# A new order for an attention and gated feed-forward kernel: how its planner prices loads and weights

## The chip, the cores and the metric

The kernel runs on one core of a Trainium2 chip. The metric is device microseconds of one execution, the median of several. Engines are named as in the profile: PE (TensorE: matrix products, with PEld for its weight loads), DVE (VectorE), ACT (ScalarE), POOL (GpSimd) and SP (SyncE, which here issues loads, DMA transposes and stores). Each engine carries out its own instructions in order, and waits on semaphores for the others.

## The reference

Causal attention with 16 extra keys and values ahead of the sequence ("beacons"), over 8 batches, 8 heads, 576 positions and 64 columns a head, and then a gated feed-forward layer (FFN) over the 4608 tokens:

```python
k_all = np.concatenate([beacon_k, k], axis=2)
v_all = np.concatenate([beacon_v, v], axis=2)
scores = scale * np.matmul(q, k_all.transpose(0, 1, 3, 2))
scores = np.where(causal, -1000000000.0, scores)
a = np.exp(scores - scores.max(-1, keepdims=True))
a /= a.sum(-1, keepdims=True) + 1e-09
attn = np.matmul(a, v_all)
x = attn.transpose(0, 2, 1, 3).reshape(B * S, H * D)
gate = np.maximum(x @ w_gate, 0.0)
out = (gate * (x @ w_val)) @ w_out
```

The weights are 512 x 1536 (gate and value) and 1536 x 512 (out). Inputs and output are float32 in HBM; products are in bf16 with float32 sums.

## The kernel before, in words

**Loads and casts.** A batch is brought in with 15 loads on SP's queue, named in strings like `ORDER0` (batch 0), `ORDER1` (batch 1) and `ORDER` (the others): `k0` to `k3` and `q0` to `q3` are K and Q of a pair of heads, `v0` to `v4` are V by 128 rows, `F` is the first rows of Q with the beacon keys, `L` the last rows of K and Q. Loads land in staging tiles `st` (seven). A cast makes bf16 of each (`h` for K and Q, line 486; `v`, lines 440 to 442), on POOL, in batch 0 on POOL or DVE (`CASTS`). PE turns K and Q by matmuls with an identity (`turned`, line 498), and ACT or DVE evict the result into `kT` and `diag`. Q lies in `diag` in blocks with zeros, so that one matmul gives both heads' scores.

**Attention.** For each pair of heads, `tile_step` computes blocks of scores on PE (lines 656 to 664; the last rows, "F", for all pairs together, line 659), their least value with the mask on DVE (L676, L679; Q carries a negative scale), exponentials with row sums on ACT (L690), the reciprocal on DVE (L704), and the normalisation on POOL (L711). The probabilities are then transposed, on PE in batch 0 (L746) and by DMA in the others (L757), and multiplied by V (L767, on half the columns of the array for each head; L796 for F). An eviction writes the result, transposed, into `xT`, the FFN's input, which stays on the chip. Batches 0 and 1 do this in three steps (AB, C, DE), batch 2 in two (AB, CDE), the others in one.

**FFN.** `hidden` makes 12 groups for each chunk of tokens: four matmuls with the gate weights, ReLU on ACT into `g` (L838), four with the value weights, and a product on DVE into `hT` (L842). `project` makes the output with 12 matmuls a tile (L854) in three parts, an eviction into `osb`, and a store. A batch's first 512 tokens go in one or two chunks (`CUTS`); the other 64 of each batch are gathered for four batches at a time.

**Weights.** The nine weights (g0, v0, g1, v1, g2, v2, o0, o1, o2, 1 MB each in HBM) are brought in, cast to bf16 on the way, by DMAs that POOL issues (L455) among its other instructions. Batch 1 and later batches may begin to load only when one weight, `GATE`, has landed; for batch 1 this is a true semaphore, on SP.

**The order.** All of this is entered as tasks with a cost, engines, dependencies, tiles that they hold and a priority. `Plan.order` takes the tasks one by one: the one that can begin first, by the planner's own model of the engines and of DMA, and at equal times by priority (`RANK`, `AHEAD`, `STEPS`, `F_RANK`, `WHOLE`, `HOLD`, `PACE`). Tasks with two engines go to the one that is free sooner. That sequence is the program: each engine's instructions stand in it as the planner took them, while the semaphores come from the true dependencies. A wrong cost therefore gives no wrong result, only another order. While PE would wait in the first microseconds, the planner puts fillers into its order (line 918): matmuls of 256 columns on constant data that nobody reads, which keep its clock up. They are part of the program and are carried out whether PE would have waited or not.

**The model of DMA before.** `wire` is when the loads' queue will be done; each load adds its move time. Weights are due `W_FROM + W_STEP * i`; while any is under way, a load is made slower by `PACKET` for each of its packets, and the weight by `W_DELAY`.

## Time and profile before

| | us |
|---|---|
| median of 3 runs (406.59 to 407.25) | 407.08 |
| the profiled execution: whole time | 407.43 |
| its span, from the first to the last instruction | 405.6 |
| PE busy, of the span | 393.0 |
| DVE busy | 314.6 |
| ACT busy | 289.8 |
| POOL busy | 232.6 |

A row of a timeline reads: start, duration, engine, line, operation, tile written <- tiles read, shape, count, and in brackets the idle time ahead of it with the engine and line that ended it. Matmuls overlap, so that the duration of one is its latency, and the distance between two starts is what it takes of PE. A row of the stretches reads: the stretch, its length, then busy time and (count) of PE, PEld, DVE, ACT and POOL, the granted share of PE's clock, the busy share of the DMA engines, and GB/s. In a row of groups, the busy time and the mean duration in ns are followed by the idle time ahead and what ended it.

### The profile page before, as it was taken

The numbers are of one execution on the slowest core, as the hardware profiler recorded it, in microseconds if no ns is written. First come the engines' busy times: TensorE is split into PE (matmuls) and PEld (weight loads), VectorE is DVE, ScalarE is ACT, GpSimd is POOL, SyncE is SP. The second block draws the span as 40 slices with busy tenths as digits, with TensorE's granted clock in tenths as the row PEclk, the third lists the DMA queues.
The fourth block names the chain that finished last, engine by engine and source line by source line (L and its number), as shares of the span: only waits on it lengthen the run. The fifth ranks groups of instructions, "written<-read, shape, count | busy, mean of one in ns | idle before, by whom it ended". The sixth has DMA issues, their size and how long they took to land.

```text
span 405.6 us, 10379 instructions
## 1 busy us (share of the span) xinstructions
PE 393.0 (97%) x3276; PEld 246.9 (61%) x3311; DVE 314.6 (78%) x1159; ACT 289.8 (71%) x959; POOL 232.6 (57%) x434
## 2 busy tenths in 40 slices
PE   7899999999999999998999999999999999999996
PEld 5567868587766877554557754554554545444484
DVE  6898999889989988898998998887988634233252
ACT  6899989789888968796888789998858433033030
POOL 5799876957786758686975965885736300000000
PEclk9999999999999999999999999999999999999999
DMA  8999999999899998999999999999296640110112
GB/s 223 170 202 224 210 216 198 195 239 204 187 182 241 199 191 222 190 225 202 236 199 210 230 203 174 256 181 222 81 163 126 146 95 0 53 52 0 53 52 54
DMA packets 172616, 68.03 MB, mean 168 GB/s; under 512 B 146832, under 2 KB 168080, under 8 KB 172560
## 3 DMA queue, kind: packets, MB, share of 16 engines
q1 hardware_dynamic: 167568, 62.38, 76.2%
q0 software_dynamic: 4752, 4.72, 7.2%
q8 instruction: 26, 0.43, 0.5%
q14 instruction: 30, 0.25, 0.2%
q10 hardware_dynamic: 240, 0.26, 0.2%
HBM read 38.27 MB, written 9.44 MB: 118 GB/s over the span
## 4 chain that ended last, share of the span: by engine, by line
PE 85%; POOL 6%; ACT 2%; DMA 2%; DVE 2%; issue 1%; SPq 0%; POOLq 0%; ACTq 0%; DVEq 0%
PE f L834 43%; PE f L854 22%; PE f L664 7%; PE f L767 5%; PE f L498 4%; POOL xT L711 2%; DMA st<-in_q_dram 2%; PE f L656 2%; POOL pb L711 1%; PE f L796 1%; POOL h L486 1%; PE f L746 1%; DVE diag L440 1%; PE f L659 1%; ACT xT L690 1%
## 5 line engine op out<-in xcount | busy, mean ns | idle before, releaser
L711 POOL TENSOR_SCALAR pb<-pb,small 128x576 bf16<-128x576 bf16 (+8 forms) x224 | 121.5, 557 | 55.4 <-DVE small L704 47.7
L690 ACT ACTIVATE pb<-f,small 128x64 bf16<-128x64 f32 (+6 forms) x256 | 131.0, 524 | 18.1 <-DVE small L679 14.3
L838 ACT ACTIVATE g<-f 128x512 f32<-128x512 f32 (+3 forms) x156 | 72.0, 470 | 66.8 <-PE f L834 65.6
L679 DVE CUSTOM_DVE_ANT_0 f<-f,mask 128x128 f32<-128x128 f32 (+7 forms) x256 | 111.8, 476 | 9.0 <-PE f L664 5.9
L834 PE MATMUL f<-xT,wv_r 128*128 128x512 bf16 (+3 forms) x616 | 111.8, 313 | 0.6
L842 DVE TENSOR_TENSOR hT<-g,f 128x512 bf16<-128x512 f32 (+3 forms) x156 | 80.1, 519 | 38.3 <-PE f L834 35.2
L834 PE MATMUL f<-xT,wg_r 128*128 128x512 bf16 (+3 forms) x619 | 109.5, 313 | 0.3
L854 PE MATMUL f<-wo_r,hT 128*128 128x512 bf16 (+1 forms) x423 | 101.9, 373 | 1.0
L834 PEld LDWEIGHTS <-wg_r 128*128 128x128 bf16 x624 | 60.0, 98 | 32.3 <-issue 0.2
L834 PEld LDWEIGHTS <-wv_r 128*128 128x128 bf16 x624 | 59.4, 98 | 32.9 <-issue 0.8
L854 PEld LDWEIGHTS <-hT 128*128 128x128 bf16 x444 | 41.6, 98 | 38.9
L690 ACT ACTIVATION_READ_ACCUMULATOR pb<-f,small 128x1 f32 x256 | 53.8, 210 | 0.0
L664 PE MATMUL f<-kT,diag 128*128 128x384 bf16 (+7 forms) x255 | 46.9, 286 | 2.2 <-DVE diag L440 1.0
L679 DVE DVE_READ_ACCUMULATOR2_ANT small<- 128x1 f32 x296 | 41.2, 139 | 0.2 <-issue 0.2
L486 POOL TENSOR_SCALAR h<-st 128x512 bf16<-128x512 f32 x62 | 37.7, 615 | 3.7 <-DMA st<-in_q_dram 1.0
L440 DVE COPY osb<-f 128x512 f32<-128x512 f32 (+1 forms) x26 | 17.6, 677 | 23.2 <-PE f L854 22.7
L711 POOL TENSOR_SCALAR xT<-xT,small 128x64 bf16<-128x64 bf16 (+4 forms) x64 | 26.9, 436 | 9.8 <-ACT xT L690 4.0
L498 PE MATMUL f<-ident,h 128*128 128x128 bf16 (+3 forms) x320 | 28.0, 218 | 2.1 <-POOL h L486 1.8
L664 PEld LDWEIGHTS <-diag 128*128 128x128 bf16 x256 | 20.4, 98 | 15.2 <-issue 1.6
L438 ACT CAST diag<-f 64x512 bf16<-64x512 f32 (+2 forms) x52 | 23.0, 443 | 9.3 <-PE f L498 4.1
L498 PEld LDWEIGHTS <-h 128*128 128x128 bf16 (+1 forms) x320 | 20.9, 99 | 13.9 <-POOL h L486 6.7
L440 DVE CAST diag<-f 64x512 bf16<-64x512 f32 (+2 forms) x44 | 26.3, 598 | 3.7 <-ACT diag L438 2.0
(67 smaller groups left out, 376.9 us busy)
## 6 DMA issues: line engine op xcount, KB each, us to landing
st<-in_q_dram SPq DMA_DIRECT2D x32, 256.0 KB, 4.4
st<-in_k_dram SPq DMA_DIRECT2D x32, 256.0 KB, 4.7
out_dram<-osb SPq DMA_DIRECT2D x32, 256.0 KB, 2.6
st<-in_v_dram SPq DMA_DIRECT2D x24, 256.0 KB, 4.8
st<-in_v_dram SPq DMA_DIRECT2D x8, 224.0 KB, 5.2
wg_r<-in_moe_w_gate_dram POOLq DMA_DIRECT2D x3, 512.0 KB, 8.7
wv_r<-in_moe_w_val_dram POOLq DMA_DIRECT2D x3, 512.0 KB, 9.9
wo_r<-in_moe_w_out_dram POOLq DMA_DIRECT2D x3, 512.0 KB, 13.3
```

The source lines that it names most:

```text
L438: nc.scalar.copy(dst, src)
L440: nc.vector.tensor_copy(dst, src)
L486: (nc.gpsimd if x.engine == "POOL" else nc.vector).tensor_scalar(to, of, by, 1.0, ALU.mult, ALU.mult)
L498: nc.tensor.matmul(to, h16.tile[:deep, a * P:(a + 1) * P], ident[:deep, :rows], start=True, stop=True)
L664: nc.tensor.matmul(view(i), t.diag.tile[:, p, j * P:j * P + P], kT[:, p, :n], start=True, stop=True)
L679: nc.vector.tensor_tensor_reduce(out=view(i), in0=view(i), in1=msk, scale=1.0, scalar=small["t"][:, 0:1] if name in "EF" else 3.0e38, op0= ...
L690: nc.scalar.activation(ph.tile.rearrange("p a n -> p (a n)")[:, a:a + n], view(i), AF.Exp, bias=small["t"][:, low:low + 1], scale=-1.0, ac ...
L711: (nc.gpsimd if x.engine == "POOL" else nc.vector).tensor_scalar(one, one, small["t"][:, 8 + i:9 + i], 1.0, ALU.mult, ALU.mult)
L834: nc.tensor.matmul(to, w_r[:, ki, nf * P:(nf + 1) * P], x, start=(ki == 0), stop=(ki == KM - 1))
L838: r = add("ACT", c_act(w), lambda _, psg=psg, g=g: nc.scalar.activation(g.tile[:, :w], psg.tile[:, :w], AF.Relu), (a,), (psg, g), -1000 + ...
L842: hid.append(add("DVE", c_dve(w), lambda _, psv=psv, g=g, nf=nf: nc.vector.tensor_mul(hT[nf].tile[:, c0:c0 + w], g.tile[:, :w], psv.tile[: ...
L854: nc.tensor.matmul(ps.tile[:, :w], hT[nf].tile[:, t0:t0 + P], wo_r[:, nf, n0:n0 + w], start=(nf == 0), stop=(nf == NF - 1))
```

## The change

What is computed does not change, nor any instruction's shape but those named here. The change replaces the planner's model of DMA, refits many of its costs, and takes new values for all priorities, so that the order of nearly all instructions is another.

- A class `Wire` models the loads' queue and the weights' queue: alone, a load takes its move time and a weight `W_MOVE`; together they take turns packet by packet (a weight has `W_PACKETS`). A weight's arrival is now taken from this, and tasks behind it become ready when it lands (`LANDING` after its last packet).
- Each weight has its own earliest time, `W_AT`, in place of `W_FROM + W_STEP * i`.
- Behind 60 us of planned time, each signal to a task takes 0.3 us more for PE and 0.15 for others (`SLACK`).
- In the model, F's value products are no longer of the kind that shares a tiling with the others, and F's scores are a kind of their own.
- Fillers multiply a tile of ones, written by DVE at the start, in place of identity and mask, which POOL writes; they may begin at 0.95 instead of 1.55, and until 8 us they fill a wait of PE wholly, later three quarters of it.
- Casts of batch 0 go to POOL alone; `GATE` is g1 instead of g0; the cut of batch 1's first chunk is at 368 tokens instead of 240; scores may hold five PSUM banks instead of four (`SC_MOST`), batch 0's turns and values six instead of four (`FIRST_MOST`).
- `SLOT_LAZY` and the second value of `begin` are gone; evictions of one tile's two halves are chained in the plan.

```diff
-W_FROM = 14.62
-W_STEP = 2.67
+W_AT = (13.08, 14.33, 19.39, 19.58, 33.69, 35.02, 39.54, 43.52, 48.0)
...
-GATE = ('g', 0)
-SC_MOST = 4
+GATE = ('g', 1)
+SC_MOST = 5
...
-ORDER0 = "q0 q1 F k0 k1 k3 v1 q3 k2 q2 v2 v3 L v0 v4"
-ORDER1 = "k0 F q0 k2 L k3 q2 v3 q3 k1 v0 v2 q1 v1 v4"
-ORDER = "q0 k1 L k0 F q3 k3 q1 v1 k2 v0 v4 v3 q2 v2"
+ORDER0 = "k3 k0 k2 v4 F q0 q3 k1 q1 L q2 v2 v1 v0 v3"
+ORDER1 = "k1 q0 F k2 q2 v4 q3 v1 v0 q1 k0 v3 v2 k3 L"
+ORDER = "k1 v1 q2 k0 k3 q0 F q1 q3 v4 k2 L v2 v3 v0"
...
-CASTS = ('POOL', 'DVE')
+CASTS = ('POOL',)
...
-CUTS = {0: (240,), 1: (240,), 2: (240,), 3: ()}
+CUTS = {0: (240,), 1: (368,), 2: (240,), 3: ()}
...
+class Wire:
...
+    def load(self, at, move, packets):
+        self.idle_to(at)
+        left = 1.0
+        beside, slower = move + packets * W_MOVE / W_PACKETS, W_MOVE + W_PACKETS * move / packets
+        while left > 1e-9:
+            w = self.weights[self.next] if self.next < len(self.weights) else None
+            if w is None or w[1] >= self.at + left * move:
+                self.at += left * move
+                left = 0.0
+            elif w[1] > self.at:
+                left -= (w[1] - self.at) / move
+                self.at = w[1]
+            elif w[2] * slower <= left * beside:
+                left -= w[2] * slower / beside
+                self.at += w[2] * slower
+                w[2], w[3] = 0.0, self.at
+                self.next += 1
+            else:
+                w[2] -= left * beside / slower
+                self.at += left * beside
+                left = 0.0
+        return self.at
...
+                              + (0.0 if end <= SLACK_FROM else SLACK[0] if "PE" in u.engines else SLACK[1]))
...
-                n = int((at - since) * FILL / 0.107) if at > WARM else int((at - since) * FILL0 / 0.2137)
+                rate = 0.2137 if since < WARM else 0.107
+                n = int((at - since) * FILL / 0.107) if at > FILL_COLD else math.ceil((at + FILL_PAD - since) / rate) if at > since else 0
...
+    def make_ones(_):
+        nc.vector.memset(ones, 1.0)
...
-        weight(kind, j, -21.0 + 0.1 * i, W_FROM + W_STEP * i)
+        weight(kind, j, -21.0 + 0.1 * i, W_AT[i])
...
-            nc.tensor.matmul(to[:, :256], ident, mask.bitcast(BF16)[:, :256], start=True, stop=True)
+            nc.tensor.matmul(to[:, :256], ones[:, :P], ones, start=True, stop=True)
```

## The prediction, as put on record before the changed kernel ran

> **What bounds the kernel now.** I read the page's busy line and slices first, then the chain of waits, then the busy time by stretch.

> ```profile
> span 405.6 us, 10379 instructions
> PE 393.0 (97%) x3276; PEld 246.9 (61%) x3311; DVE 314.6 (78%) x1159; ACT 289.8 (71%) x959; POOL 232.6 (57%) x434
> PE   7899999999999999998999999999999999999996
> PE 85%; POOL 6%; ACT 2%; DMA 2%; DVE 2%; issue 1%; SPq 0%; POOLq 0%; ACTq 0%; DVEq 0%
> ```
> ```profile
> 0.00:28.64 28.64, 24.07 (x221) 16.90 (x222) 24.07 (x119) 22.86 (x74) 21.65 (x49) 1.00 0.96 194
> 28.64:45.00 16.36, 15.79 (x221) 12.15 (x220) 14.54 (x55) 15.20 (x46) 16.18 (x27) 1.00 1.20 223
> 45.00:300.00 255.00, 251.88 (x2226) 164.16 (x2251) 228.31 (x869) 216.63 (x750) 183.04 (x339) 1.00 1.04 202
> 300.00:405.60 105.60, 101.30 (x611) 53.72 (x618) 47.64 (x118) 35.16 (x93) 11.76 (x22) 1.00 0.28 68
> L918 PE MATMUL f<-mask,ident 128*128 128x256 bf16 x90 | 15.5, 305 | 1.9 <-POOL mask L383 1.9
> ```

> TensorE (PE) is the bound, and its true work is the same in both kernels: the order of instructions holds the same 3221 matmuls beside the fillers (90 before, 105 after). So only three things can change: the time until PE has FFN matmuls to fill its waits with, the small costs between matmuls, and PE's waits. After 28.64 us PE idles 0.57 us until 45 and 3.12 us (255.00 - 251.88) until 300. The start is where time is lost: PE is called busy for 24.07 of 28.64 us, but most of that is fillers.

> ```profile
> 1.89 2.50 PE L918 MATMUL f<-mask,ident 128*128 128x256 bf16 x11 [1.89 <-POOL mask L383]
> 5.71 1.70 PE L918 MATMUL f<-mask,ident 128*128 128x256 bf16 x7
> 8.09 0.39 PE L498 MATMUL f<-ident,h 128*128 128x128 bf16 x4
> 8.31 0.49 PE L918 MATMUL f<-mask,ident 128*128 128x256 bf16 x3
> 8.64 0.39 PE L498 MATMUL f<-ident,h 128*128 128x128 bf16 x4
> 9.35 0.73 PE L664 MATMUL f<-kT,diag 128*128 128x64 bf16 x6 [0.32 <-ACT kT L438]
> 28.64 0.57 PE L834 MATMUL f<-xT,wg_r 128*128 128x240 bf16 x4
> ```

> A matmul's own duration is its latency; what it takes of PE is the distance to the next start. Three fillers of 256 columns take 0.33 us (8.31 to 8.64), so 0.107 each or 2400 columns per us; I count PE's work that way, with a pair of half-width value products as one. Before the first FFN matmul at 28.64 stand 8.19 us of true work, so 20.45 us are lost there.

> **The change part by part.** The change redraws the whole order, so I sum by stage.

> *A. Until the first FFN matmul.* The order of after puts 8.53 us of true work and 11.09 us of fillers (104) ahead of it. Its first scores need q0, now the sixth load (behind k3, k0, k2, v4 and F); before, q0 came first and their last load, k0, fourth. On PE, 43 fillers (4.59 us) and 1.39 us of turns stand ahead of these scores. The first eleven fillers above start every 0.21 us (1.89 to 4.18), double the 0.107 of 8.31, and the slow spacing still holds in the seven from 5.71. If PE is slow until 7.5 us as there, a start near 1.05 us (the fillers now wait for a memset on DVE alone) does 6.45 / 2 = 3.2 us of that work by 7.5, the other 2.75 by 10.25. So the first score comes no sooner than about 10.3, against 9.35.

> [...]

> ```profile
> 10.82 0.32 ACT L690 ACTIVATE xT<-f,small 128x64 bf16<-128x64 f32 x1
> 15.48 0.58 ACT L438 CAST diag<-f 64x512 bf16<-64x512 f32 x1 [1.46 <-DVE diag L440]
> 29.48 0.47 ACT L838 ACTIVATE g<-f 128x240 f32<-128x240 f32 x1
> L690 ACT ACTIVATE pb<-f,small 128x512 bf16<-128x512 f32 x4 | 2.9, 719 | 0.0
> L690 ACT ACTIVATE pb<-f,small 128x448 bf16<-128x448 f32 x2 | 1.3, 658 | 0.0
> L438 ACT COPY xT<-f 128x768 bf16<-128x768 bf16 x1 | 0.8, 819 | 0.0
> ```

> Then ACT sets the pace. From its first exponential (10.82) to its first ReLU (29.48) it took 18.66 us, 17.2 without the 1.46 wait for DVE. The order of after has 38 instructions there too: one exp of 512, one of 448 and one copy of 768 more (0.72 + 0.66 + 0.82), one exp of 320 less (some 0.55), and smaller evictions of K and Q (some 0.65 less): together about 1.0 more, 18.2. Its first exp I put 0.8 later, at 11.6: the scores are 0.95 later, ACT's own evictions ahead of them end nearer to them. 11.6 + 18.2 = 29.8 without a wait, 0.3 later than before, so FFN starts near 29.0. PE has then done 0.34 more true work. A = 0.3 - 0.34, taken as 0. Bounds: -0.5 (exp at 11.1) to +1.5 (a wait like the 1.46 again). What speaks for no wait: K and Q of all four pairs are now loaded and turned ahead of V, and DVE, whose eviction ACT waited for, loses four casts.

> ```profile
> L486 DVE TENSOR_SCALAR h<-st x2: 383/404/426, 3.7 to 9.0; 128x512 bf16<-128x512 f32 x2
> L486 POOL TENSOR_SCALAR h<-st x62: 607/617/620, 4.6 to 286.3; 128x512 bf16<-128x512 f32 x62
> ```

> Those casts (two of h, two of v) cost POOL 4 x 0.62 = 2.5 us. POOL was busy 21.65 of 28.64 us, so 7 us of idle time hide them; without that cover they would add up to 2.5.

> *B. Batch 1's loads behind the third weight.* Before, every load of batch 1 waited for the first weight (GATE g0), now for g1. SP is in order, so behind that wait stand all further loads, the transposes and the output stores.

> ```profile
> 16.04 0.93 POOL L455 DMA_DIRECT2D wg_r<-in_moe_w_gate_dram  x1
> 19.64 0.79 POOL L455 DMA_DIRECT2D wv_r<-in_moe_w_val_dram  x1
> 21.93 0.79 POOL L455 DMA_DIRECT2D wg_r<-in_moe_w_gate_dram  x1
> DMA to landing us min/median/max: 5.7/8.7/10.7
> DMA to landing us min/median/max: 6.0/9.9/12.4
> st<-in_k_dram SPq DMA_DIRECT2D x32, 256.0 KB, 4.7
> 37.93 0.39 PE L498 MATMUL f<-ident,h 128*128 128x128 bf16 x4
> ```

> The two landing rows (least, median, most) are the gate weights' and the value weights'. Before, g0 (issue 16.04, landed 5.7 later, 21.75) let the loads go, and PE asked for batch 1's first turn only near 37.9: some 11 us of cover. In after that turn stands 1.12 us of true work behind the first FFN matmul, near 30.2. On POOL stand ahead of g1 ten casts of Q and K and three of V (13 x 0.62 = 8.1), eight normalisations of 0.29 to 0.45 (3.0) and two issues (1.7); with the setup (until 3.6) and half of POOL's former waits I put its issue at 19.5. It lands at 25.2 (5.7) at best, at 28.2 (8.7, what the third weight took before) at worst; I take 6.0, the second weight's, as most of the wire is free by then: 25.5. A load of 4.7 and a cast of 0.62 with 0.1 of signal: 30.9 against 30.2. But a first FFN matmul that is itself a little late hides some, so B = +0.4; bounds 0 and 28.2 + 5.4 - 30.2 = +3.4 (5.4 being the same load and cast).

> *C. Changes of array tiling.* Value products run on half the columns, F's scores on a quarter. The row shapes of PE show what going in and out costs:

> ```profile
> 30.64 0.57 PE L834 MATMUL f<-xT,wg_r 128*128 128x240 bf16 x4
> 31.14 0.36 PE L767 MATMUL f<-xT,v 128*64 128x128 bf16 x6
> 36.19 0.53 PE L767 MATMUL f<-xT,v 128*64 128x128 bf16 x12
> 36.65 0.39 PE L918 MATMUL f<-mask,ident 128*128 128x256 bf16 x2
> ```

> Four of 240 columns from 30.64 end at 31.04, the next starts at 31.14: 0.10. Six pairs of 128 from 36.19 end at 36.51, the next starts at 36.65: 0.14. The order holds 60 such changes before and 67 after: C = 7 x 0.11 = +0.8 (0.7 to 1.0).

> *Batch 1's cut.* 240 + 272 columns become 368 + 144: the same columns and as many instructions. A 144-column matmul takes 0.060, and a turn of 128 with its own weights takes 0.055 (8.09 to 8.31), so weight loads hide: 0. Were they to show at 98 ns each, 96 x 0.038 = 3.6.

> *D. PE's waits behind the start.*

> ```profile
> 38.55 0.29 PE L498 MATMUL f<-ident,h 128*128 128x64 bf16 x4 [0.23 <-POOL h L486]
> 60.69 0.40 PE L498 MATMUL f<-ident,h 128*128 128x128 bf16 x4 [0.58 <-POOL h L486]
> 188.93 0.32 PE L498 MATMUL f<-ident,h 128*128 128x80 bf16 x4 [0.98 <-POOL h L486]
> DMA to landing us min/median/max: 5.4/10.6/14.8
> DMA to landing us min/median/max: 10.7/11.9/13.4
> ```

> The two last rows are loads of Q, K and V issued in 21 to 30 and in 37 to 50 us: with weights on the wire all that time they landed after 10.6 and 11.9 (medians) where 4.7 is usual, and the waits named at 38.55 and 60.69 are turns whose casts came late. After spaces its weights: 23 instructions of POOL, of 0.3 to 0.7 us each, stand between the fourth and the fifth, so for some 8 us the loads should have the wire alone and take about 4.7; the plan also allows 0.3 us more on each signal to PE behind 60 us. Of the idle 0.57 + 3.12 = 3.7 I take 2.4 as gained. Bounds: all 3.7 gained; or 1.6 lost, new waits as long as the two later ones here (0.58 + 0.98) on top of the old, since batch 2's first turn moves from 48.6 to 40.3 us of true work and so nearer to its loads.

> *End.* The last value product has 57 us of true work behind it before, 59 after, and the same last evictions and stores: 0.

> Sum: 0 + 0.4 + 0.8 - 2.4 = -1.2. The profiled execution took 407.43 us (span 405.6, 1.83 around it); the median is 407.08, 0.35 lower. 407.08 - 1.2 = 405.9; I say 405.8, as a part of B goes if A comes out late.

> **Rivals.**
> 1. *The gate decides (slower).* g1 lands near 28.2, PE stands at batch 1's first turn, which is in order ahead of all FFN work. For it: its cover of 11 us falls to none, and the third weight took 8.7. Against: batch 0's loads end sooner than batch 1's did, so less shares the wire. It decides from a landing past 27.3 (B = 2.5, so 408.0); at worst B = 3.4 and the time 408.9.
> 2. *Waits only change place.* D gains 1 instead of 2.4 and C stays: 407.08 + 0.4 + 0.8 - 1.0 = 407.3, no change. For it: PE idles only 1% already, and new orders bring new tight places.
> 3. *Vector work comes too early (slower).* Batch 7's first turn moves from 224 to 206 us of true work, so DVE (228.31 of 255 busy) must go faster on the way, and POOL takes casts. Each missed turn costs 0.6 to 1; D = +1.6 gives 409.9.
> 4. *The start gains too* (A = -0.5, B = 0, D = -3.7): 403.7.

> **How the numbers follow.** The forecast has 0.42, rival 1 0.25, rival 2 0.14, rival 3 0.12, rival 4 0.07. A measurement of this kernel can tell about 0.2%, 0.8 us, from no change. Faster: 0.42 + 0.07 = 0.49; same 0.14; slower 0.37. The forecast's own range is 404.2 to 406.2; for 8 in 10 it reaches to most of rivals 1 and 3 and to rival 4: 403.3 to 409.6.

> **What would show it.** First score (the six matmuls on kT and diag) at 10.2 to 10.8, first exp near 11.6, first FFN matmul at 28.5 to 29.5 (A). SP's wait for g1 ending at 25 to 26, and PE idle ahead of a turn between 29 and 32 of under 1 us (B); 2 us or more there is rival 1. Batch 1's K and Q loads landing in about 5 us, PE's idle time between 45 and 300 near 1.5 (D); over 3 us there is rival 2 or 3. I am wrong altogether if the first FFN matmul comes past 31, or if PE's idle time is less and the span is not.

## The result, and the profile after

| | before | after |
|---|---|---|
| median, us | 407.08 (406.59 to 407.25) | 409.15 (408.23 to 410.52, 5 runs) |
| ratio of after to before, 95% interval | | 1.0054 (1.0028 to 1.0079) |
| the profiled execution: whole time | 407.43 | 408.32 |
| its span | 405.6 | 406.3 |

The change makes the kernel slower by half a per cent, 2.1 us; forecast were 405.8 us, 1.2 us less than before. The profiled execution of after is 0.8 us below its median, that of before 0.35 above: the two traces show only 0.7 us of the 2.1, and the rest lies in executions that these two traces don't show.

The head of the page, its slices of PE and its chain, and then the busy time by stretch (stretch, length, busy time and count of PE, PEld, DVE, ACT, POOL, granted clock, DMA share, GB/s):

```profile
span 406.3 us, 10439 instructions
PE 395.8 (97%) x3326; PEld 245.1 (60%) x3326; DVE 310.5 (76%) x1151; ACT 288.8 (71%) x964; POOL 236.0 (58%) x438
PE   7999999999999999999999999999999999999995
PE 87%; DMA 5%; POOL 2%; ACT 2%; DVE 1%; issue 1%; SPq 0%; POOLq 0%
```
```profile
28.64:45.00 16.36, 15.54 (x207) 11.93 (x202) 14.87 (x54) 15.15 (x48) 15.01 (x25) 1.00 1.11 222
45.00:300.00 255.00, 254.63 (x2280) 161.88 (x2278) 225.19 (x867) 216.40 (x756) 184.52 (x340) 1.00 1.03 202
```

PE is the bound as before: the chain of waits is PE's for 87% (85 before). It idles 0.82 us of the second stretch (0.57 before), and 0.37 us between 45 and 300, where it idled 3.12 before. That looks like a gain of 2.7, but the two figures can't be set against each other: after has as many matmuls as weight loads (3326), before has 3276 against 3311, so 35 records are missing there (25 of them between 45 and 300), and a missing matmul reads as idle time. What can be compared is the time at which the same amount of true work is done, as in the prediction. These are the rows of the start: PE, then ACT, then POOL, then SP's wait.

```profile
1.25 4.18 PE L996 MATMUL f<-ones 128*128 128x256 bf16 x19 [1.25 <-DVE scales L492]
5.26 0.61 PE L570 MATMUL f<-ident,h 128*128 128x128 bf16 x8
...
11.58 0.40 PE L570 MATMUL f<-ident,h 128*128 128x128 bf16 x4
...
11.93 0.84 PE L742 MATMUL f<-kT,diag 128*128 128x64 bf16 x6
...
29.68 0.55 PE L845 MATMUL f<-pTb,v 128*64 128x192 bf16 x10
30.17 1.06 PE L912 MATMUL f<-xT,wg_r 128*128 128x240 bf16 x8
31.06 0.50 PE L824 MATMUL f<-ident,xT 128*128 128x128 bf16 x6
32.12 0.40 PE L570 MATMUL f<-ident,h 128*128 128x128 bf16 x4 [0.56 <-POOL h L558]
```
```profile
13.75 0.31 ACT L768 ACTIVATE xT<-f,small 128x64 bf16<-128x64 f32 x1
31.46 0.72 ACT L916 ACTIVATE g<-f 128x240 f32<-128x240 f32 x2
```
```profile
6.47 0.62 POOL L558 TENSOR_SCALAR h<-st 128x512 bf16<-128x512 f32 x1 [1.32 <-DMA st<-in_k_dram]
7.88 0.62 POOL L514 TENSOR_SCALAR v<-st 80x512 bf16<-80x512 f32 x1 [0.79 <-DMA st<-in_v_dram]
8.72 0.69 POOL L558 TENSOR_SCALAR h<-st,scales 64x512 bf16<-64x512 f32 x1 [0.23 <-DMA st<-in_beacon_k_dram]
9.38 1.32 POOL L558 TENSOR_SCALAR h<-st 128x512 bf16<-128x512 f32 x2
20.47 0.79 POOL L527 DMA_DIRECT2D wg_r<-in_moe_w_gate_dram  x1
31.45 0.62 POOL L558 TENSOR_SCALAR h<-st 128x512 bf16<-128x512 f32 x1 [0.78 <-DMA st<-in_k_dram]
```
```profile
SPq L593 <- DMA wg_r<-in_moe_w_gate_dram: 12.2, 1, 12.2
```

- *Start.* The first score is at 11.93, the first exponential at 13.75 (10.82 before), the first FFN matmul at 30.17 (28.64 before). With the 8.53 us of true work ahead of it, 21.64 us are lost there against 20.45: +1.2.
- *Batch 1's first turn.* SP waited 12.2 us for g1, issued at 20.47; it landed 6.3 us later, the first load went out at 26.87, and its cast began at 31.45. PE's six transposes from 31.06 take 0.33, and the turn comes at 32.12: +0.7 (the row's own 0.56 counts from the end of the last one's latency).
- *Later.* The last eviction of an output tile begins at 401.55, against 401.82 before (rows below). So PE is 0.3 us ahead at the end, and between the first turn of batch 1 and the end it won 2.2 us, the changes of tiling included.
- *End.* Yet the span is 0.7 longer. These are the last evictions and stores, of before and of after:

```profile
400.08 0.69 DVE L440 COPY osb<-f 128x512 f32<-128x512 f32 x1 [2.97 <-PE f L854]
400.51 0.37 ACT L438 COPY osb<-f 128x256 f32<-128x256 f32 x1 [3.95 <-PE f L854]
400.79 1.95 SPq L867 DMA_DIRECT2D out_dram<-osb  x3
400.80 2.07 ACTq L867 DMA_DIRECT2D out_dram<-osb  x3
401.82 0.42 DVE L440 COPY osb<-f 128x256 f32<-128x256 f32 x1 [1.05 <-PE f L854]
```
```profile
400.67 0.69 DVE L512 COPY osb<-f 128x512 f32<-128x512 f32 x1 [3.85 <-PE f L932]
401.11 0.37 ACT L510 COPY osb<-f 128x256 f32<-128x256 f32 x1 [4.83 <-PE f L932]
401.39 1.79 SPq L945 DMA_DIRECT2D out_dram<-osb  x3
401.39 2.07 ACTq L945 DMA_DIRECT2D out_dram<-osb  x3
401.55 0.43 DVE L512 COPY osb<-f 128x256 f32<-128x256 f32 x1 [0.18 <-PE f L932]
```

Before, two of the three last tiles are evicted 1.3 us ahead of the third, and their stores have been issued when the third is ready: ACT issues its third and last store at 402.3, at once. After, the tiles' products are done side by side, all three evictions fall within 0.9 us, the third tile's stores have to wait for the four ahead of them, and ACT issues the last one at 402.9. From the end of the last eviction to the end of the span: 405.6 - 402.24 = 3.36 before, 406.3 - 401.98 = 4.32 after: +1.0.

The sum of the trace: 1.2 + 0.7 - 2.2 + 1.0 = +0.7, the difference of the spans.

### The profile page after: what moved, and what is told of

Its sections match the earlier page's. It is cut to its first block, busy times and chain, and to the rows that moved or that the text cites. A ratio compares the mean times of both kernels' runs of the same rounds, so it can differ in the third digit from the quotient of the medians.

```text
span 406.3 us, 10439 instructions
## 1 busy us (share of the span) xinstructions
PE 395.8 (97%) x3326; PEld 245.1 (60%) x3326; DVE 310.5 (76%) x1151; ACT 288.8 (71%) x964; POOL 236.0 (58%) x438
## 4 chain that ended last, share of the span: by engine, by line
PE 87%; DMA 5%; POOL 2%; ACT 2%; DVE 1%; issue 1%; SPq 0%; POOLq 0%
PE f L912 45%; PE f L932 23%; PE f L742 7%; PE f L845 5%; PE f L570 4%; DMA st<-in_k_dram 3%; DMA wo_r<-in_moe_w_out_dram 2%; PE f L734 2%; ACT xT L768 1%; PE f L874 1%; POOL h L558 1%; PE f L737 1%; POOL xT L789 1%; PE f L824 1%; ACT diag L510 0%
## 5 line engine op out<-in xcount | busy, mean ns | idle before, releaser
L789 POOL TENSOR_SCALAR pb<-pb,small 128x320 bf16<-128x320 bf16 (+8 forms) x224 | 122.3, 560 | 68.6 <-DVE small L782 49.8
L768 ACT ACTIVATE pb<-f,small 128x64 bf16<-128x64 f32 (+7 forms) x256 | 132.2, 533 | 15.5 <-DVE small L757 11.1
L916 ACT ACTIVATE g<-f 128x512 f32<-128x512 f32 (+5 forms) x156 | 71.8, 476 | 68.1 <-PE f L912 64.8
L757 DVE CUSTOM_DVE_ANT_0 f<-f,mask 128x512 f32<-128x512 f32 (+7 forms) x256 | 112.1, 475 | 4.7 <-PE f L742 3.4
L912 PE MATMUL f<-xT,wv_r 128*128 128x512 bf16 (+5 forms) x624 | 111.8, 314 | 0.0
L920 DVE TENSOR_TENSOR hT<-g,f 128x512 bf16<-128x512 f32 (+5 forms) x156 | 80.1, 521 | 39.2 <-PE f L912 37.2
L912 PE MATMUL f<-xT,wg_r 128*128 128x512 bf16 (+5 forms) x624 | 109.3, 313 | 0.0
L742 PE MATMUL f<-kT,diag 128*128 128x512 bf16 (+7 forms) x256 | 46.3, 286 | 0.3
L754 DVE TENSOR_REDUCE small<-f 128x1 f32<-128x512 f32 x40 | 27.3, 683 | 4.0 <-PE f L734 2.9
L768 ACT ACTIVATE xT<-f,small 128x64 bf16<-128x64 f32 (+3 forms) x64 | 27.8, 457 | 0.2
## 6 DMA issues: line engine op xcount, KB each, us to landing
st<-in_k_dram SPq DMA_DIRECT2D x32, 256.0 KB, 4.6
st<-in_q_dram SPq DMA_DIRECT2D x32, 256.0 KB, 4.7
out_dram<-osb SPq DMA_DIRECT2D x32, 256.0 KB, 2.6
st<-in_v_dram SPq DMA_DIRECT2D x24, 256.0 KB, 5.4
```

The costliest lines, as they stand in the source:

```text
L742: nc.tensor.matmul(view(i), t.diag.tile[:, p, j * P:j * P + P], kT[:, p, :n], start=True, stop=True)
L754: nc.vector.tensor_reduce(out=to, in_=view(i), axis=AX.X, op=ALU.min)
L757: nc.vector.tensor_tensor_reduce(out=view(i), in0=view(i), in1=msk, scale=1.0, scalar=small["t"][:, 0:1] if name in "EF" else 3.0e38, op0= ...
L768: nc.scalar.activation(ph.tile.rearrange("p a n -> p (a n)")[:, a:a + n], view(i), AF.Exp, bias=small["t"][:, low:low + 1], scale=-1.0, ac ...
L789: (nc.gpsimd if x.engine == "POOL" else nc.vector).tensor_scalar(one, one, small["t"][:, 8 + i:9 + i], 1.0, ALU.mult, ALU.mult)
L912: nc.tensor.matmul(to, w_r[:, ki, nf * P:(nf + 1) * P], x, start=(ki == 0), stop=(ki == KM - 1))
```

## The experiments

In these kernels the plan's finished order is kept and only the named tasks are moved in it, or the semaphore that batch 1's first loads wait for is another. `put(a, b)` moves task a directly ahead of task b; a load is ("ld", batch, piece), a cast ("cast", batch, piece), a third of an output tile's product ("out", token, column, third), its eviction "ev", a half of its store "st". Kernels with the same third column ran beside the kernel before on one chip; chips differ by up to 1 us, so the ratios are what to compare. Most have 12 runs, a_gatev1 has 6, a_idle3, a_idle6 and a_wpack have 4. The ratio is formed over all these runs and is not the quotient of the two medians (for a_same that would be 1.0054).

| kernel | median, us | before beside it | ratio (95% interval) |
|---|---|---|---|
| a_same: the change's kernel again | 408.70 | 406.51 | 1.0041 (1.0020 to 1.0063) |
| a_tail: old end | 407.47 | 406.51 | 1.0009 (0.9990 to 1.0029) |
| a_v4late: V's last rows late | 407.75 | 406.51 | 1.0022 (1.0004 to 1.0039) |
| a_gate0: gate on g0 | 408.39 | 406.51 | 1.0027 (1.0009 to 1.0045) |
| b_tail: before with the new end | 407.98 | 407.22 | 1.0017 (1.0001 to 1.0033) |
| a_v4tail: late V, old end | 407.68 | 407.22 | 1.0004 (0.9988 to 1.0020) |
| a_all: late V, old end, gate on v0 | 406.70 | 407.22 | 0.9983 (0.9967 to 0.9999) |
| a_gatev1: gate on v1 | 410.07 | 407.22 | 1.0070 (1.0044 to 1.0096) |
| a_early: a_all, loads ahead of transposes | 406.37 | 406.37 | 1.0004 (0.9989 to 1.0018) |
| a_idle3: a_gate0, 3 copies on POOL | 409.23 | 406.37 | 1.0061 (1.0038 to 1.0083) |
| a_idle6: a_gate0, 6 copies on POOL | 412.87 | 406.37 | 1.0158 (1.0140 to 1.0176) |
| a_wpack: g2, v2 right behind v1 | 414.46 | 406.37 | 1.0199 (1.0177 to 1.0222) |
| a_three0: late V, old end, gate on g0 | 406.21 | 406.45 | 0.9992 (0.9978 to 1.0006) |
| a_early0: a_three0, loads ahead of transposes | 405.84 | 406.45 | 0.9986 (0.9974 to 0.9998) |

**The change's kernel again (a_same).**

> The changed kernel once more, unchanged, as the base of this set. Its five times lay between 408.23 and 410.52, while the kernel before kept within 0.7 us. If the spread is the chip's, the kernel before shows it here too; if it is the new order's, a median near 409 and a spread of 2 us come back, and a slower execution's trace should show one wait on PE that the first trace (408.32) had small: I suspect the wait for the last output weight, 0.3 us there.

The loss comes back: 1.0041. The spread is not the new order's own: the copy's times lie between 407.37 and 410.86, those of the kernel before beside it between 405.42 and 408.96 over 35 runs. The copy's profiled execution took 410.49 us, and shows what the quick one did not, at another place than the output weight that I suspected: the first row is PE's first turn of batch 1, the second POOL's cast for it, the others are windows of 1 us.

```profile
33.56 0.40 PE L573 MATMUL f<-ident,h 128*128 128x128 bf16 x4 [2.41 <-ACT xT L775]
```
```profile
32.89 0.62 POOL L559 TENSOR_SCALAR h<-st 128x512 bf16<-128x512 f32 x1 [2.67 <-DMA st<-in_k_dram]
```
```profile
31.00:32.00 1.00, 0.15 (x3) 0.00 (x0) 0.52 (x4) 1.00 (x5) 0.00 (x0) 1.00 0.56 121
32.00:33.00 1.00, 0.00 (x0) 0.00 (x0) 0.00 (x0) 1.00 (x4) 0.11 (x1) 1.00 0.74 229
33.00:34.00 1.00, 0.44 (x7) 0.43 (x7) 0.01 (x1) 0.52 (x2) 0.78 (x2) 1.00 1.02 329
34.00:35.00 1.00, 1.00 (x10) 0.85 (x8) 0.99 (x2) 0.00 (x0) 1.00 (x2) 0.68 0.96 217
35.00:36.00 1.00, 1.00 (x13) 0.64 (x12) 0.41 (x1) 0.00 (x0) 1.00 (x3) 0.50 1.10 256
...
37.00:38.00 1.00, 1.00 (x15) 0.41 (x13) 0.51 (x2) 0.98 (x2) 1.00 (x2) 0.62 1.17 193
```

Here g1, issued at 20.06, landed 7.9 us later; the loads went out at 27.97 and the cast could begin at 32.89. PE waited 2.41 us (the row names ACT, whose part had long been done; the cast came last), and then the granted clock was 0.50 from about 34.4 to 37.8: PE shows as busy, but 13 transposes take 1.50 us of it (35.88 to 37.38), where in a_tail, at a clock of 1.00, they take 0.83 (34.40 to 35.23). At 56 us of the trace this execution is 2.5 us behind the quick one. So batch 1's turn costs 0.7 us in one execution and some 3 us more than that in another.

How often the clock falls can be read from the record, which has each execution's mean granted clock. A stretch of 3.4 us at 0.50 takes 0.004 from that mean. Of the 17 executions of this kernel (5 of after, 12 of a_same) the one shown has 0.993 and the others have 0.997 to 1.000; the longest two, 410.86 and 410.52 us, have 0.998 and 1.000. So the halved clock is not what makes the slow executions slow, and what does is open.

**The end (a_tail, b_tail).** In the first the old order is put back into the change's kernel, in the second the new one into the kernel before. The lines with a minus are the order of the change, those with a plus the old one:

```diff
-("out", 128, 256, 0), ("out", 0, 0, 1), ("out", 128, 0, 1), ("out", 128, 256, 1), ("out", 0, 0, 2), ("out", 128, 0, 2),
-("ev", 0, 0), ("out", 128, 256, 2), ("ev", 128, 0), ("ev", 128, 256), ("st", 0, 0, 64), ("st", 0, 0, 0),
+("out", 0, 0, 1), ("out", 128, 0, 1), ("out", 0, 0, 2), ("out", 128, 0, 2), ("ev", 0, 0), ("out", 128, 256, 0),
+("ev", 128, 0), ("st", 0, 0, 64), ("st", 0, 0, 0), ("out", 128, 256, 1), ("st", 128, 0, 0), ("st", 128, 0, 64),
+("out", 128, 256, 2), ("ev", 128, 256),
...
```

> The changed kernel with the kernel before's order of its last output products: each tile's parts are finished one tile after the other instead of side by side, with the same work. Theory (the end costs): PE ends at the same time, the last stores are issued one instead of three deep on each queue, and the span ends about 0.7 to 0.9 us sooner: the time falls by 0.6 to 0.9. Rival (the last landing is noise of that one execution): no change, within 0.2.

> The kernel before with one thing of the change alone: its last output products, evictions and stores in the order that the change gives them (parts of the three last tiles side by side, all three evictions last). Theory 1 (the end costs by itself, since three stores deep stand on SP's and ACT's queues behind the last evictions): +0.7 to +1.2 us on the kernel before, with PE's last matmul where it was and the last stores' issues 0.4 to 0.7 later. Rival (the 1.2 us that the change's kernel gained with the old end came from run to run differences): within 0.3 us of the kernel before.

The old end gains 0.32% of the ratio (1.2 us of the median, more than expected), though its interval and the copy's overlap; the new end costs the kernel before 0.17% (0.8 us, as expected). The traces agree with each other better than the medians do. The last eviction of b_tail (span 406.1 us), and then that of a_tail (span 406.0):

```profile
401.31 0.42 DVE L440 COPY osb<-f 128x256 f32<-128x256 f32 x1 [0.18 <-PE f L861]
```
```profile
402.18 0.42 DVE L512 COPY osb<-f 128x256 f32<-128x256 f32 x1 [1.05 <-PE f L939]
```

From the end of the eviction to the end of the span: 4.37 with the new order in the old kernel, 3.40 with the old order in the new one, against 3.36 and 4.32. The end costs 1.0 us by itself, in both kernels.

**The start (a_v4late).** V's last rows of batch 0, loaded and cast fourth in the change's order, go behind the first Q and K, with a staging tile of their own:

```diff
+seq[where("ld", 0, "v4")].holds[0].tile = cp.tile([P, DM], FP32, name="stx")
+put(("ld", 0, "v4"), ("ld", 0, "v3"))
+put(("cast", 0, "v4"), ("cast", 0, "v0"))
```

> The changed kernel with one load and its cast moved: V's last rows of batch 0 (80 rows of short pieces, fourth in the queue) go behind the other loads of V, in a staging tile of their own; all else stays in its place. Theory (the first scores wait for the loads ahead of q0): first score 0.7 to 1.0 us sooner than 11.93, first exp likewise, first FFN matmul near 29.4 instead of 30.17. PE then stands longer at batch 1's first turn, which is tied to g1's landing, so only 0 to 0.4 us of it reaches the end. Rival (POOL's casts in a row set the start): first score within 0.2 of 11.93.

```profile
12.40 0.31 ACT L775 ACTIVATE xT<-f,small 128x64 bf16<-128x64 f32 x1
```
```profile
29.10 0.99 PE L919 MATMUL f<-xT,wg_r 128*128 128x240 bf16 x8
```

The first exponential comes 1.35 us sooner, the first FFN matmul 1.07, and PE's last matmuls still 1.1 sooner. The times say 0.19% (0.95 us of the median), more than I had expected, but the two intervals overlap, so that the trace carries this more than the times. So loads and casts ahead of q0 hold the first exponential, and ACT passes it on to FFN. The edit moves a load and its cast together and can't tell which of them it is; and 12.40 is still 1.6 later than the 10.82 of before, for which no run was made.

**The gate (a_gate0, a_gatev1).** The order is the same; only the semaphore differs.

```diff
-one.ins, weight_dma[GATE].ins.name
+one.ins, weight_dma["g", 0].ins.name
```

> The changed kernel with the same order, but batch 1's loads wait for the first weight's landing instead of the third's. Theory (the gate's cost is PE's wait of 0.7 us at batch 1's first turn): the loads are issued near 21.8 instead of 26.87, that wait goes, and the time falls by 0.4 to 0.7. Rival (loads beside the weights delay the weights): g1 and v1 land 2 to 4 us later, at 29 to 34, the FFN groups on them wait, and nothing is gained or the time rises.

> The change's kernel with the loads of batch 1 held until the fourth weight has landed, one weight later than in the change; all else as in the change. Its issue is 1.4 us later and its landing 2 to 3 us later. Theory 1 (the gate decides, and a PE wait of over 2 us is followed by a halved clock for some 4 us): PE waits 3.0 to 5.0 us at batch 1's first turn, the granted clock reads about 0.5 for the 3 to 4 us behind it in every execution, and the time is 411.5 to 414. Theory 2 (the wait costs only its own length, and the low clock seen in one execution was by chance): +2.0 to +3.0 us on the unchanged copy, 410.7 to 411.5, with a clock of 1.00. Rival (the wait is absorbed by later waits of PE): within 1 us of the unchanged copy.

With the gate on g0, the loads go out at 21.90 and PE comes to batch 1's first turn at 31.46 without a wait; the same score matmul that starts at 74.47 in the quick execution of after starts at 73.55. But then these turns of batch 2 and 3 wait, and the load of K that the first of them needs was issued no sooner than in after (PE's rows and SP's row of a_gate0, then SP's row of after):

```profile
94.66 0.40 PE L573 MATMUL f<-ident,h 128*128 128x128 bf16 x4 [0.41 <-POOL h L559]
103.90 0.40 PE L573 MATMUL f<-ident,h 128*128 128x128 bf16 x4 [0.44 <-POOL h L559]
```
```profile
88.76 0.51 SPq L596 DMA_DIRECT2D st<-in_k_dram  x1
```
```profile
88.32 1.09 SPq L593 DMA_DIRECT2D st<-in_k_dram  x1
```

The turn at 94.66 starts only 0.35 sooner than in after, the one at 103.90 is 0.27 later: the gain of 0.9 is used up in this execution, and the times show 0.14% (0.3 to 0.6 us), which is not clear of noise. With the gate on v1 the ratio is 0.3% above the copy's and the time, 410.07, below what each of the two theories had. Its one profiled execution was the quickest of the six and had a wait of 1.75 with the clock at 1.00; two of the other five have a mean clock of 0.994 and 0.996, while the rest have 0.998 and more: the clock did not fall "in every execution", which theory 1 had expected. The next pair tells the theories apart.

**The price of a wait (a_idle3, a_idle6).** On a_gate0, with extra copies on POOL ahead of batch 1's first cast (six are shown, a_idle3 has three):

```diff
+for _ in range(6):
+    nc.gpsimd.tensor_scalar(scratch, mask, 1.0, 1.0, ALU.mult, ALU.mult)
 cast(x)
```

> The change's kernel with the early gate (no wait of note at batch 1's first turn) and, to price a wait there by its length, three extra copies of 128x512 on POOL into an unused tile ahead of batch 1's first cast, about 1.8 us. Theory 1 (a wait of under 2 us costs its length and no more): PE waits 1.6 to 2.0 us at that turn with the clock at 1.00 behind it; PE is 1.6 to 2.0 us later than without the copies at 74 us and 0.7 to 1.1 later from 110 us on (0.9 is room that the loads of batch 2 leave). Rival (any wait over 1 us lowers the clock): the clock reads under 1.0 in 34 to 38 us and PE is over 3 us later at 74 us.

> The same with six extra copies, about 3.7 us. Theory 1 (a wait of over 2 us is followed by a granted clock of 0.5 for about 3.5 us): PE waits 3.4 to 3.8 us, the clock reads 0.5 to 0.6 in the four us behind it, PE is 5.0 to 5.6 us later than without the copies at 74 us, and 4 to 4.7 later at the end: 412 to 413.5. Theory 2 (the low clock in one execution was not the wait's): PE is 3.4 to 3.8 us later at 74 us and 2.5 to 2.9 at the end, 410.8 to 411.3, with the clock at 1.00.

PE's first turn of batch 1, with three copies, and then with six and the windows behind it:

```profile
33.15 0.40 PE L573 MATMUL f<-ident,h 128*128 128x128 bf16 x4 [1.74 <-POOL h L559]
```
```profile
35.48 0.40 PE L573 MATMUL f<-ident,h 128*128 128x128 bf16 x4 [3.85 <-POOL h L559]
```
```profile
36.00:37.00 1.00, 1.00 (x9) 0.81 (x8) 0.91 (x2) 0.00 (x0) 1.00 (x3) 0.60 0.21 50
37.00:38.00 1.00, 1.00 (x13) 0.63 (x11) 0.41 (x1) 0.00 (x0) 1.00 (x3) 0.50 1.09 246
...
39.00:40.00 1.00, 1.00 (x16) 0.48 (x14) 0.53 (x3) 0.97 (x2) 1.00 (x3) 0.69 0.23 50
```

The wait of 1.74 us left the clock at 1.00 and put PE 1.5 us later than in a_gate0 at 55 us; that of 3.85 was followed by a clock of 0.50 for 3.4 us and put PE 5.3 us later, 1.5 more than the wait. At the end of the span 0.5 and 4.0 are left, the first a little less than expected. The mean clock is 0.992 to 0.996 in all four executions of a_idle6 and 0.997 to 0.999 in those of a_idle3. So theory 1 holds for both: it was the wait that lowered the clock. That its length alone decides is not shown (see the last section).

**Weights beside batch 1's loads (a_wpack).**

```diff
+at = where("w", "v", 1)
+two = [seq.pop(where("w", "g", 2)), seq.pop(where("w", "v", 2))]
+seq[at + 1:at + 1] = two
```

> The change's kernel with the third gate and value weights (g2, v2) issued straight behind the second ones, 14 us sooner, so that weights are on the wire while batch 1's loads run, as in the kernel before. Theory 1 (batch 1's loads land in 4.4 to 5.7 us because no weight shares the wire then): they land after 7 to 12 us instead, PE waits 4 to 9 us in all at batch 1's turns, 411 to 416 us. Rival (the loads land as fast as their own queue lets them): 4.4 to 6 us as before, PE waits no more than in the unchanged copy, 408 to 409.5.

The loads issued behind the gate, KB each and median us to landing, in after (26 to 36 us) and then in a_wpack (26 to 45):

```profile
st<-in_q_dram SPq DMA_DIRECT2D x3, 256.0 KB, 5.2
st<-in_k_dram SPq DMA_DIRECT2D x2, 256.0 KB, 4.7
```
```profile
st<-in_q_dram SPq DMA_DIRECT2D x4, 256.0 KB, 9.2
st<-in_k_dram SPq DMA_DIRECT2D x3, 256.0 KB, 7.4
```

PE waited 3.93 us at batch 1's first turn, where theory 1 had 4 to 9 at all of its turns, and then had a clock of 0.50 for nearly 7 us:

```profile
36.41 0.61 PE L573 MATMUL f<-ident,h 128*128 128x128 bf16 x4 [3.93 <-POOL h L559]
```

The time is 2% above the kernel before, as theory 1 had it. Spacing the weights is what lets batch 1's loads land in about 5 us.

**All together (a_v4tail, a_all, a_early, a_three0, a_early0).** a_all holds batch 1 on v0. In the two early kernels loads go ahead of the transposes behind which they stood (K of pair 2 with V's last rows and L of batch 2, K of pair 1 of batch 3; in a_early0 also the three of batch 3 that correspond to the first three). `turns` are the transposes, named by their planned start:

```diff
+behind([t for t in turns if 79.0 < t.start < 79.2][0], ("ld", 2, "v4"), ("ld", 2, "k2"), ("ld", 2, "L"))
+behind([t for t in turns if 91.5 < t.start < 91.7][0], ("ld", 3, "k1"))
```

> The change's kernel with two parts put back: V's last rows of batch 0 loaded and cast behind the first Q and K, and the old order of the last output products. Alone they gained 0.95 and 1.2 us on the unchanged copy (408.7). Theory 1 (the start and the end are separate costs and add): 406.5 us or a little above, the same as the kernel before; first exponential near 12.4, first FFN matmul near 29.1, a wait of 1 to 2 us at batch 1's first turn still there. Rival (what is gained at the start is given back later in waits for the loads of batch 2, as in the run with the early gate, which gained 0.9 us by 74 us and lost 1.2 again between 94 and 133): 407.3 to 407.8, with waits for casts between 94 and 133 us of over 0.8 us.

> The same two parts put back and the loads of batch 1 held only until the second weight has landed instead of the third. Theory 1 (three separate costs): no wait over 0.6 us at batch 1's first turn, no lower clock there, 405.3 to 406.2 us, faster than the kernel before (406.5) by 0.3 to 1.2. Rival (the wait changes place): the wait at batch 1's first turn is gone, waits of about 1 us for casts of batch 2 stand between 94 and 133 us in its place, and the time is that of the same kernel with the late gate, within 0.3 us.

> The version with three parts put back (V's last rows late, the old end, the gate on the second weight), and now four loads of batches 2 and 3 (V's last rows, K of pair 2 and the last rows of batch 2; K of pair 1 of batch 3) ahead of one or two transposes on SP's queue instead of behind them: some 8 and 3 us sooner. Theory 1 (what PE gained before 88 us is lost in two waits for these loads, at 93.4 and 102.6 us, since SP reaches them no sooner than 88 and 96 however early PE is): the two waits go, PE is 0.6 to 1.1 us ahead of that version from 107 us on, 405.6 to 406.2 us against its 406.7 (0.9960 to 0.9975 of the kernel before). Rival (SP's transposes or the wire hold the loads, or the later transposes cost the value products as much): the waits move to products that need the transposed tiles, and the time is within 0.3 us of the version without the move.

> The change's kernel with V's last rows late, the old end, and batch 1's loads held until the first weight has landed, as in the kernel before. Theory 1 (the change's loss was these three): PE's wait at batch 1's first turn is under 0.5 us; two to three waits of 0.3 to 0.6 us for casts at 93 to 133 us take back about 1 us; 0.9965 to 0.9985 of the kernel before. Rival (what is won at batch 1's turn is lost at batch 2's in full): 0.999 to 1.001.

> The same, with seven loads of batches 2 and 3 (V's last rows, K of pair 2 and the last rows of each, and K of pair 1 of batch 3) ahead of the transposes on SP's queue that they stand behind. Theory 1 (these waits are the only thing that takes the gain back): no wait over 0.2 us for a cast between 45 and 150 us, 0.6 to 1.1 us below the kernel without the move (0.994 to 0.9965 of the kernel before). Rival (another stage takes it back, or the loads' place costs the transposes): within 0.3 us of the kernel without the move.

Late V and the old end together give 1.0004, where the two gains alone add up to 0.9990; the intervals leave open whether 0.6 us is lost again or none. With an earlier gate the whole loss is gone: 0.9983 on v0, 0.9992 on g0, where the unchanged copy has 1.0041. In the profiled executions of a_early, a_three0 and a_early0 no turn waits between 45 and 150 us. But a_early, with the gate and the two parts of a_all, has 1.0004 and not the 0.9960 to 0.9975 expected: in its profiled execution PE waited 1.5 us at batch 1's first turn, since v0 landed only 10.2 us after its issue. And a_three0 kept its lead without the move, against what I expected, though its ratio lies in the rival's range. The move gains 0.4 us in the medians (406.21 to 405.84), where 0.6 to 1.1 was expected, and the intervals overlap: it is not shown to help. a_early0 is the only one of the g0 kernels whose interval lies below 1: by 0.14%.

## Why the prediction was wrong, point by point

- *A, the start (0, bounds -0.5 to +1.5): measured +1.2.* The failed step is "Its first exp I put 0.8 later, at 11.6": it came 2.9 later, at 13.75. The first score (11.93) has 1.6 of the 2.15 between 11.6 and 13.75. I counted fillers and turns ahead of it, took the 10.3 of "no sooner than" for the time itself, and did not work out when q0's data come. POOL's rows answer it: casts one by one, with 1.32, 0.79 and 0.23 us of waiting for k2, v4 and F, so that q0's cast begins at 9.38; then comes PE's turn of k1 (11.58) ahead of the score. a_v4late shows that one load and one cast less in that row gives 1.35 back; the other 1.6 were not tried. ACT's way from there was right: 17.7 us to the first ReLU, 18.2 forecast, and no wait for DVE. "PE is slow until 7.5 us" was wrong as well for this execution (eight turns of 128 columns from 5.26 take 0.45 us), and did not matter: in a_same eight such turns from 5.27 take 0.86, turns at the closer spacing come only at 7.11 (four in 0.23), and its first score at 11.69 was no later.
- *B, the gate (+0.4, bounds 0 to +3.4): +0.7 in the quick execution, 2.4 and then half a clock for 3.4 us in the other.* The mechanism is rival 1's, which had a quarter. g1's issue was put at 19.5 and came at 20.47 and 20.06; its landing, taken at 6.0, was 6.3 and 7.9. The step that failed is taking one landing near the lower end for a wait that PE has no cover for; that +0.7 lies close to +0.4 is luck of the execution that was profiled. And one price was not in the bounds: that of the clock, 1.5 (a_idle6) to 1.7 us (half of 3.4), which one of the 17 executions paid.
- *C, tiling (+0.8):* the row at 29.68 gives 0.09 for a change (ten products in five pairs of 192 columns end at 30.08, the next starts at 30.17). No run tried this term alone.
- *D, PE's later waits (-2.4):* with C at 0.8, the 2.2 won between batch 1's turn and the end make D -3.0. The kind was right, and a_wpack shows a cause: with weights on the wire batch 1's loads land in 7 to 9 us. The size is not confirmed, since -3.0 is a remainder that rests on the untested C: the waits that the traces name behind the first FFN matmul, batch 1's first turn left out, are 0.23, 0.58 and 0.98 us before and 0.18 and 0.29 after, which gives 1.3. What was wrong is the reading of 3.7 us idle as the most to be gained, since part of that was missing records.
- *End (0): measured +1.0.* The failed step is "the same last evictions and stores: 0". The instructions are the same; that three evictions now come together, with six stores behind them on two queues, is what costs. b_tail and a_tail show it from both sides.
- *The sum.* In the traces 1.2 + 0.7 + 0.8 - 3.0 + 1.0 = +0.7, forecast -1.2; A and the end are the difference, with D 0.6 better and B 0.3 worse. The other 1.4 us of the median lie in the executions: 1.2 of it is how the two profiled ones stand to their medians. A wait with a halved clock like that of a_same is not the reason for them, as one execution in 17 had it; the reason is open.
- *Rivals 2 and 3:* no vector work came too early (the one wait of PE named between 45 and 300 is 0.29 us, for a weight), and PE's waits did not just change place in after. They did in the trace of a_gate0, where a gain of 0.9 us was lost behind SP's queue.

What stays open: why g1 lands after 6.3 us in one execution and 7.9 in another, what makes executions of one kernel differ by up to 3.5 us, and whether the gains of the start and the end add in full. That the start, the gate and the end together are the loss is shown by putting back parts of all three (0.9983, 0.9992 and 0.9986, and 1.0004 in a_early with its late v0, against 1.0041); what each is worth alone rests on the traces more than on the times.

## What to carry to other kernels

The end of a kernel has its own price, which no busy share shows: look at when the last evictions come and how many stores stand ahead of the last one on each queue. A semaphore on a DMA's landing is to be priced with its latest landing (7.9 us for g1 here, not 6.3), and if the engine behind it is PE, with the clock that went to 0.50 for 3.4 us behind the waits of 2.41 and 3.85 us in a_same and a_idle6. A gain at the start can be lost at the next queue in order (here SP with its transposes and loads, in the trace of a_gate0; a_three0 kept most of its gain), so look there before counting on it; and work put ahead of the first needed tile delays everything behind it, even if it is due soon. A trace of one execution is one sample: what differs by less than the spread of a kernel's own times needs runs as well.

## What the runs showed of the hardware that was not expected

```profile
35.00:36.00 1.00, 0.00 (x0) 0.00 (x0) 0.00 (x0) 0.00 (x0) 0.27 (x1) 0.73 1.21 279
```

From the means of these windows and of those of 0.5 us, the clock was at 0.50 from 34.35 to 37.76 in a_same, from 36.20 to 39.61 in a_idle6 and from 35.46 to 42.30 in a_wpack. PE's waits had begun at 31.15, 31.63 and 32.48 (where the wait ends, less its length), so that the falls came 3.2, 4.6 and 3.0 us behind that. A wait's length alone does not give the moment of the fall, then, and what gives it these traces do not show; nor does a run show that a length between 1.75 and 2.41 us divides the two kinds of wait: the 2 us of the expectations were the author's estimate.

At the start PE's matmuls come at about half the later pace, which the granted clock of the windows does not show (1.00 from 1.0 to 5.2 us of after). There fillers start every 0.21 us (later every 0.107) until the turns of 5.26, 4.0 us after the first filler (1.25). In the kernel before this took 5.5 to 5.8 us from its first filler (1.89): seven fillers from 5.71 still take 1.66, four from 7.64 take 0.45. That need not be the kernel, as the change's kernel in its other traced execution (a_same) was slow until past 6 us (eight turns from 5.27 in 0.86) and fast only at 7.11. For the fillers' purpose, to keep the clock up, these waits speak (0.50 behind 2.41, 3.85 and 3.93 us without work, 1.00 behind 1.75 and less); no run leaves the fillers out, so what they are worth at the start is not shown.
